# A gated linear recurrence with a feed-forward layer on one core: weights loaded in six pieces, the quarter turn by a 128-row matmul, and another order table

## The chip, the core and the metric

The kernel runs on one core of one Trainium2 chip. The core has five engines that each work through a queue of their own in order: TensorE (PE, with its weight loads shown apart as PEld), VectorE (DVE), ScalarE (ACT), GpSimd (POOL) and SyncE (SP). SP issues most transfers; sixteen DMA engines carry them out. The metric is the device time of one execution in microseconds (us); a lower number is better. The median of three runs of the kernel before is 193.87 us (193.51 to 193.95). One further execution was recorded by the hardware profiler, and all durations below are from it.

## The reference

For each of 4 batches and 8 heads a state of 48 x 48 is carried over 768 steps, with a complex decay per step and row, and a layer norm with a feed-forward layer follows on the 384 channels of each token:

```
mag = sqrt(a_re^2 + a_im^2);  scale = min(mag, 0.999) / (mag + 1e-6)
for t in range(768):
    S_re, S_im = ar*S_re - ai*S_im + k[t] v[t]^T,  ar*S_im + ai*S_re
    y[t] = q[t] @ S_re                      # x: 8 heads side by side, 384 channels
xn = (x - mean(x)) / sqrt(var(x) + 1e-6) * g_ln
out = x + max(xn @ w_ch1, 0) @ w_ch2        # w_ch1 384 x 1536, w_ch2 1536 x 384
```

Inputs and output are float32.

## The kernel before, in words

**Tiling.** The 768 steps of a batch are cut into chunks of 128 steps. Two chunks make a pair, so there are 12 pairs P (three to a batch) and 24 chunks n. Step names carry these numbers: `ln.3.0` belongs to pair 3, `y.5` to chunk 5. Pair 0 is worked in two halves of four heads (`ln.0.0`, `ln.0.1`).

**The decay of a pair.** ACT takes the logarithm of a_re (`ln`, L448) and its inverse (`iv`, L450); `r` is a_im over a_re, `r2` its square, `u` a logarithm on ACT (L462), `l` and `lc` (DVE, L466 and L469) the capped logarithm of the magnitude. PE sums it over the steps with a triangle of ones (`dec`, L477), and ACT forms `e` and `en`, its exponentials (L481). The angle goes the same way: arctan on ACT (`th`, L485), summed on PE (`ph`, L492 and L496), then `sin` (L514). For pairs 0 to 3 the cosine is a sine after a quarter turn: `qt` (L521) adds 0.25 to the sum on PE with a one-row matmul. Later pairs use `abs` and a bias. `car` hands the last angle on to the next pair.

**The attention of a pair.** `qe`, `ke`, `qs`, `ks` scale q and k by these tables (DVE or POOL, L294). `qT` and `kT` transpose on PE (L593) and `qsT`, `ksT` copy the result out (L291 on DVE, L289 on ACT), or SP does both with a transposing DMA (L598). Then `am` (L616), the mask `atm` (DVE), the state `gm` and `G`, the output `y` (L666, L669) and its copy `x`, its statistics `bn`, and its transpose `xtr` and copy `xT`.

**The feed-forward of a pair.** `mm1` (L720, 6 calls of 6 matmuls), `relu` (L731 ACT, L733 DVE), `mm2` (L741, 6 calls of 4 matmuls), the scaling and sum `oa` and `ot`, and the store `st`. The norm's gain and mean are folded into the first weight matrix once at the start: `wgc` makes a matrix of the gain, `wp` (PE, L384) the column means of a third of w1b, and nine `wc` (DVE, L388) correct w1b in place. `mm1` of a third waits for its three `wc`.

**Weights.** `wl.0` (L364) and `wl.1` (L366) load the two matrices whole. POOL issues them, because the transfer casts float32 to bfloat16. They go to a DMA queue of their own, q0 in the profile; all of SP's transfers go to q1.

**Order.** Every step and its engine stand in the table `PLAN`, written out ahead of time by a planner: `name:engine`, with the PSUM bank behind the letter and, after `@`, a step of another engine that must have ended first. The kernel issues the steps in that order, so each engine's queue is the table filtered by that engine, and a step that waits holds up everything behind it on its engine. `tab.log` and `tab.trig` (L775) load the ACT tables for logarithms and exponentials, or for sine and arctan. `warm` steps (L770) are matmuls whose results nobody reads.

Of the kernel before, what the change touches and what calls it, by code (L numbers as in the profile page):

```python
# [51 lines left out]
tab.trig.1:A sin.0.0:A3 qe.0.1.0:V qe.0.0.0:V q.1.1:S mask:G ke.0.0.0:G@qe.0.0.0 ke.0.1.0:V r2.2.0:V
qs.0.0.1:V qs.0.1.1:V th.1.0:A qt.0.1:P0 warm.52:P4 warm.53:P4 warm.54:P4 warm.55:P4 warm.56:P4 warm.57:P4
warm.58:P4 warm.59:P4 warm.60:P4 warm.61:P4 warm.62:P4 warm.63:P4 warm.64:P4 warm.65:P4 warm.66:P4
warm.67:P4 warm.68:P4 warm.69:P4 qt.0.0:P3 dps.0:P2 cos.0.0:A3 cos.0.1:A0 ks.0.0.1:V ks.0.0.0:V ks.0.1.0:V
qs.0.1.0:V ph.1.0:P4 dec.1.0:P6 qs.0.0.0:V warm.70:P1 warm.71:P1 qT.1:P3 tab.log.2:A en.1.0:A6 u.2.0:A
ln.3.0:A iv.3.0:A e.1.0:A6 v.0:G@qs.0.0.0 decc.0:V2 ks.0.1.1:V vf.1.1:S vf.1.0:S q.2.0:S car.1.0:V4
warm.72:P1 warm.73:P1 kT.0:P2 qT.0:P1 kT.1:P0 qsT.1:V3 tab.trig.2:A sin.1.0:A4 ksT.0:V2 wl.0:G ksT.1:V0
am.1:P2 gm.0:P0 ke.1.0.1:G@ks.0.1.1 ke.1.0.0:G th.2.0:A qsT.0:V1 am.0:P6 dps.1:P1 decc.1:A1 qt.1.0:P4
l.2.0:V r.3.0:V lc.2.0:V G.0:V0 gm.1:P0 cos.1.0:A4 dec.2.0:P4 k.2.1:S tab.log.3:A e.2.0:A4 en.2.0:A4  # L60
atm.0:V6 atm.1:V2 G.1:V0 r2.3.0:V k.2.0:S are.4.0:S ph.2.0:P6 y.1:P1 aim.4.0:S ks.1.0.1:G@lc.2.0 x.1:V1
are.5.0:S ks.1.0.0:G y.0:P2 kT.3:P3 x.0:V2 ksT.3:V3 u.3.0:A tab.trig.3:A sin.2.0:A6 wp.2:P0 wc.2.1:V0
wc.2.0:V0 xtr.0:P1 wl.1:G xtr.1:P4 wp.0:P5 wp.1:P2 wc.2.2:V0 xT.1:V4 qt.2.0:P6 xT.0:A1 kT.2:P3 th.3.0:A
# [12 lines left out]
ph.4.0:P0 atm.4:V2 k.4.0:S y.4:P5 mm2.2.1:P4 ks.3.0.0:G ks.3.0.1:V l.4.0:V lc.4.0:V mm2.3.0:P6 mm2.3.1:P6
gm.4:P7 mm2.3.2:P6 abs.4.0:A0 sin.4.0:A0 qe.3.0.0:V qs.3.0.0:V qs.3.0.1:V dec.4.0:P2 vf.3.1:S st.0:S G.4:V7
# [138 lines left out]
def kernel(  # L216
# [590 lines left out]
```

## Time and profile before

| what | value |
|---|---|
| median of three runs | 193.87 us |
| span of the profiled execution, first to last instruction | 191.7 us |
| PE, DVE, ACT, POOL busy in it | 175.3, 154.8, 165.2, 109.2 us |
| ACT table loads | 23, 29.5 us |
| warm matmuls | 74, 10.5 us |
| start of the first `mm1` (L720) | 37.45 us |
| w1b: issue by POOL, time to landing | 22.69 us, 9.9 us |
| w2b: issue by POOL, time to landing | 31.43 us, 11.9 us |

The profiled execution gives its span and no time of its own that includes what lies around the span; the span is 2.2 us under the median of the runs. A matmul's duration in the profile includes its way through the array, so neighbours overlap; what one costs in a dense stretch is the length of the stretch over the count.

### The profile page before, as it was taken

Reading aid. Unit: us, or ns where it says so; the run is one execution under the profiler, and the core shown is the slowest. Engines: PE = TensorE matmul, PEld = TensorE weight load, DVE = VectorE, ACT = ScalarE, POOL = GpSimd, SP = SyncE. Lnnn points to the kernel's source line nnn. Section 1 sums busy time; section 2 is a strip of 40 time slices with the busy share of each in tenths; the row PEclk is TensorE's granted clock in tenths of the full one; section 3 lists DMA queues with packets and bytes.
Section 4 is the critical chain, followed back from the end, with each engine's and each line's share of the span. In section 5 each row is a group of like instructions: output and inputs, shape, how many; then the busy total and the mean of one; then the engine's idle time right before and its main releaser. Section 6 shows DMA issues by size and latency. Waiting matters only on the chain.

```text
span 191.7 us, 5125 instructions
## 1 busy us (share of the span) xinstructions
PE 175.3 (91%) x2039; PEld 132.7 (69%) x2039; DVE 154.8 (81%) x267; ACT 165.2 (86%) x234; POOL 109.2 (57%) x124
## 2 busy tenths in 40 slices
PE   5567958999999989999999999999999999999991
PEld 3355644577786777787686877868777678787760
DVE  2369996999999998799999989997987484868612
ACT  3999999989999999999799988999999989427540
POOL 8601449927695599652496764585495857600500
PEclk9999996999999999999999999999999999999997
DMA  6999999999899979999899996999998979996033
GB/s 151 291 244 219 236 190 203 168 218 298 184 212 237 166 163 255 192 258 211 161 169 265 167 255 152 184 288 253 204 228 153 208 145 144 248 103 165 3 129 118
DMA packets 132104, 37.56 MB, mean 196 GB/s; under 512 B 127088, under 2 KB 131696, under 8 KB 132080
## 3 DMA queue, kind: packets, MB, share of 16 engines
q1 hardware_dynamic: 130128, 34.88, 87.7%
q0 software_dynamic: 1952, 2.36, 7.3%
q8 instruction: 16, 0.26, 0.5%
q14 instruction: 8, 0.07, 0.1%
HBM read 28.31 MB, written 4.72 MB: 172 GB/s over the span
## 4 chain that ended last, share of the span: by engine, by line
PE 38%; ACT 27%; DVE 16%; issue 8%; DMA 4%; POOL 3%; SPq 1%; DVEq 0%; POOLq 0%; ACTq 0%
PE banks L741 14%; PE banks L720 9%; ACT h L731 5%; ACT L775 4%; DVE w1b L388 3%; DMA qsT<-qs 3%; PE banks L477 2%; PE banks L616 2%; DVE l L466 2%; ACT r L462 2%; ACT en L481 2%; PE banks L496 2%; PE banks L593 2%; ACT r L458 2%; DMA are<-in_a_re_dram 2%
## 5 line engine op out<-in xcount | busy, mean ns | idle before, releaser
L741 PE MATMUL banks<-w2b,h 128*128 128x384 bf16 x288 | 54.9, 326 | 0.3 <-ACT h L731 0.2
L720 PE MATMUL banks<-xT,w1b 128*128 128x256 bf16 x432 | 51.9, 272 | 0.8 <-ACT trig L514 0.5
L720 PEld LDWEIGHTS <-w1b 128*128 128x128 bf16 x432 | 41.2, 98 | 7.7 <-DVE xT L291 1.3
L741 PEld LDWEIGHTS <-h 128*128 128x128 bf16 x288 | 26.0, 97 | 14.3 <-ACT h L731 0.8
L294 DVE TENSOR_TENSOR atm<-banks,mask 128x1024 bf16<-128x1024 f32 x24 | 28.7, 1217 | 5.2 <-PE banks L616 2.8
L731 ACT ACTIVATE h<-banks 128x1024 bf16<-128x1024 f32 x24 | 24.1, 1023 | 8.7 <-PE banks L720 8.5
L775 ACT ACT_TABLE_LOAD x23 | 29.5, 1283 | 1.2 <-PEq L791 0.8
L294 POOL TENSOR_TENSOR ks<-ke,trig 128x768 bf16<-128x768 bf16 x14 | 22.8, 1640 | 8.8 <-DVE ke L294 2.8
L294 POOL TENSOR_TENSOR qs<-qe,trig 128x768 bf16<-128x768 bf16 x11 | 18.0, 1641 | 12.3 <-DVE ot L755 5.0
L294 POOL TENSOR_TENSOR ke<-k,en 128x384 bf16<-128x384 f32 x18 | 16.5, 930 | 11.8 <-DMA vf<-in_v_dram 10.3
L294 POOL TENSOR_TENSOR qe<-q,e 128x384 bf16<-128x384 f32 x16 | 14.6, 921 | 12.2 <-ACT e L481 5.9
L733 DVE TENSOR_SCALAR h<-banks 128x1024 bf16<-128x1024 f32 x12 | 14.5, 1215 | 4.9 <-PE banks L720 4.9
L753 POOL TENSOR_TENSOR ot<-ot,x 128x384 f32<-128x384 f32 x8 | 7.3, 916 | 14.6 <-ACT ot L746 13.6
L616 PE MATMUL banks<-qsT,ksT 128*128 128x128 bf16 x192 | 14.3, 219 | 1.4 <-DVE ksT L291 1.2
L616 PEld LDWEIGHTS <-ksT 128*128 128x128 bf16 x192 | 12.1, 98 | 3.4 <-DVE ksT L291 1.4
L496 PE MATMUL banks<-th,u_th 128*128 128x384 f16 (+1 forms) x52 | 12.4, 325 | 2.2 <-ACT th L485 2.2
L679 DVE BATCH_NORM_STATS2 stats<-x 128x6 f32<-128x384 bf16 x24 | 13.1, 547 | 0.0
L755 DVE SCALAR_TENSOR_TENSOR ot<-banks,rstd,x 128x384 f32<-128x384 f32 x16 | 9.6, 609 | 4.1 <-DMA out_dram<-ot 2.9
L466 DVE SCALAR_TENSOR_TENSOR l<-r,w 128x768 f16<-128x768 f16 (+1 forms) x13 | 11.5, 892 | 1.6 <-ACT r L462 1.6
L770 PE MATMUL banks<-u_e 128*128 128x256 f16 x74 | 10.5, 302 | 2.2 <-POOL u_e L328 2.2
L477 PE MATMUL banks<-l,u_e 128*128 128x384 f16 (+1 forms) x52 | 10.4, 327 | 2.2 <-DVE l L469 1.3
L448 ACT ACTIVATE w<-are 128x768 f32<-128x768 f32 (+1 forms) x13 | 10.3, 796 | 2.2 <-DMA are<-in_a_re_dram 2.2
(96 smaller groups left out, 372.1 us busy)
## 6 DMA issues: line engine op xcount, KB each, us to landing
q<-in_q_dram SPq DMA_DIRECT2D x24, 192.0 KB, 4.0
k<-in_k_dram SPq DMA_DIRECT2D x24, 192.0 KB, 4.1
vf<-in_v_dram SPq DMA_DIRECT2D x24, 192.0 KB, 4.2
out_dram<-ot SPq DMA_DIRECT2D x24, 192.0 KB, 2.9
are<-in_a_re_dram SPq DMA_DIRECT2D x11, 384.0 KB, 4.4
aim<-in_a_im_dram SPq DMA_DIRECT2D x11, 384.0 KB, 4.5
w1b<-in_moe_w_ch_dram POOLq DMA_DIRECT2D x1, 1152.0 KB, 9.9
w2b<-in_moe_w_ch_dram POOLq DMA_DIRECT2D x1, 1152.0 KB, 11.9
```

Source lines behind the costliest of these rows:

```text
L294: {"DVE": nc.vector, "POOL": nc.gpsimd}[eng(name)].tensor_tensor(**kw)
L466: nc.vector.scalar_tensor_tensor(out=S_("l"), in0=S_("r2"), scalar=0.5, in1=S_("w"), op0=ALU.mult, op1=ALU.add)
L477: nc.tensor.matmul(heads(ps[:, c]), lhsT=u_e[:, c, j], rhs=step(T("l", P), j), start=(j == 0), stop=(j == R - 1))
L496: nc.tensor.matmul(heads(ps[:, c]), lhsT=u_th[:, c, j], rhs=step(T("th", P), j), start=False, stop=(j == R - 1), skip_group_check=True)
L616: nc.tensor.matmul(ps[:, h], lhsT=T("ksT", n)[:, h], rhs=T("qsT", n)[:, h], start=True, stop=True)
L679: nc.vector.bn_stats(out=T("stats", n), in_=T("x", n))
L720: nc.tensor.matmul(ps[:, jj], lhsT=w1b[:, dc, ts(gi * JG + jj, C)], rhs=T("xT", P)[:, dc].rearrange("p c t -> p (c t)"), start=(dc == 0), ...
L731: act(out=dst, in_=src, func=AF.Relu)
L733: nc.vector.tensor_scalar(out=dst, in0=src, scalar1=0.0, scalar2=None, op0=ALU.max)
L741: nc.tensor.matmul(bank(f"o.{n}")[:, 0:DM], lhsT=T("h", P)[:, j, ts(c, C)], rhs=w2b[:, j], start=(j == 0), stop=(j == NJ - 1))
L770: g.add(f"warm.{i}", lambda i=i: nc.tensor.matmul(bank(f"warm.{i}")[:, 0:256], lhsT=u_e[:, 0, 0], rhs=u_e[:, 1].rearrange("p j t -> p (j t ...
L775: g.add(f"tab.{nm}.{i}", lambda tab=tab: nc.scalar.preload_act_table_set(tab))
```

## The change

There are three edits in the code and a new table. The two weight loads become six: `wl.0` to `wl.2` load thirds of w1b (512 columns each), `wl.3` to `wl.5` thirds of w2b. `wp.i` now waits for its own third, and `mm2.n.i` for its own. The quarter turn uses all 128 rows of `pick` and `qrow`, and `qrow` is zero but for its row HALF, which takes one more memset. The table has 137 `warm` steps for 74, 15 table loads for 23, and the other steps in another order, some on other engines: among others 31 `relu` on ACT (24 before), 19 `ks` on DVE (12), 7 `r2` on DVE (4), 27 transposing DMAs (25), and 21 `qT` and `kT` on PE (23).

```
-    g.add("qrow", lambda: nc.gpsimd.memset(qrow[ds(HALF, 1)], 0.25), needs=["ue"])
+    g.add("qrow", lambda: [nc.gpsimd.memset(qrow, 0.0), nc.gpsimd.memset(qrow[ds(HALF, 1)], 0.25)],
+          needs=["ue"])
-    g.add("wl.0", lambda: nc.gpsimd.dma_start(
-        out=w1b, in_=moe_w_ch1.rearrange("(dc p) j -> p dc j", p=C)))
-    g.add("wl.1", lambda: nc.gpsimd.dma_start(
-        out=w2b, in_=moe_w_ch2.rearrange("(jc p) e -> p jc e", p=C)))
+    for i in range(NG):
+        g.add(f"wl.{i}", lambda i=i: nc.gpsimd.dma_start(
+            out=w1b[:, :, ts(i, 512)], in_=moe_w_ch1.rearrange("(dc p) j -> p dc j", p=C)[:, :, ts(i, 512)]))
+        g.add(f"wl.{NG + i}", lambda i=i: nc.gpsimd.dma_start(
+            out=w2b[:, ts(i, JG)], in_=moe_w_ch2.rearrange("(jc p) e -> p jc e", p=C)[:, ts(i, JG)]))
-        g.add(o, wp, needs=["wgc", "wl.0"], ps=(o, 1))
+        g.add(o, wp, needs=["wgc", f"wl.{jb}"], ps=(o, 1))
-                        nc.tensor.matmul(ps[:, c], lhsT=pick[ds(HALF, 1)], rhs=qrow[ds(HALF, 1), 0:W],
+                        nc.tensor.matmul(ps[:, c], lhsT=pick, rhs=qrow[:, 0:W],
-                    needs=[f"relu.{P}.{part}", "wl.1"] + ([f"mm2.{n}.{part - 1}"] if part else []),
+                    needs=[f"relu.{P}.{part}", f"wl.{NG + part}"] + ([f"mm2.{n}.{part - 1}"] if part else []),
-    for i in range(240):
+    for i in range(137):
```

The table itself is replaced as a whole. This is what each queue does up to about the first `mm1`, taken from the old and the new table by filtering them by engine (bank numbers left out):

```
ACT before: tab.log.0 ln.1.0 iv.1.0 ln.0.0 iv.0.0 ln.0.1 iv.0.1 tab.trig.0 th.0.1 r2.0.0 th.0.0 sin.0.1
  tab.log.1 u.0.0 u.0.1 u.1.0 ln.2.0 iv.2.0 en.0.0 en.0.1 e.0.1 e.0.0 tab.trig.1 sin.0.0 th.1.0 cos.0.0 cos.0.1
  tab.log.2 en.1.0 u.2.0 ln.3.0 iv.3.0 e.1.0 tab.trig.2 sin.1.0 th.2.0 decc.1 cos.1.0 tab.log.3 e.2.0 en.2.0 u.3.0
  tab.trig.3 sin.2.0 xT.0 th.3.0 cos.2.0
ACT after:  tab.log.0 ln.0.1 iv.0.1 ln.0.0 iv.0.0 u.0.1 u.0.0 ln.1.0 e.0.1 iv.1.0 ln.2.0 en.0.1 iv.2.0 e.0.0
  u.1.0 en.0.0 tab.trig.1 th.0.0 th.0.1 th.1.0 sin.0.0 sin.0.1 th.2.0 cos.0.0 cos.0.1 tab.log.2 u.2.0 ln.3.0 e.1.0
  iv.3.0 en.1.0 tab.trig.3 sin.1.0 th.3.0 cos.1.0 tab.log.4 e.2.0 u.3.0 ln.4.0 en.2.0 iv.4.0 tab.trig.5 sin.2.0
  x.1 xT.0 sin.3.0 cos.2.0
DVE after:  uth r.0.1 r2.0.1 r.0.0 r2.0.0 l.0.1 lc.0.1 l.0.0 lc.0.0 r.1.0 r2.1.0 r.2.0 wgc l.1.0 r2.2.0 lc.1.0
  qe.0.1.0 qe.0.0.0 ke.0.1.0 ke.0.0.0 car.0.0 car.0.1 ks.0.0.1 ks.0.1.1 qs.0.1.1 wc.0.0 wc.0.2 wc.1.0 wc.1.1 wc.0.1
  l.2.0 qs.0.0.1 car.1.0 lc.2.0 qsT.0 decc.0 ksT.0 decc.1 ksT.1 wc.2.1 wc.1.2 wc.2.0 atm.0 qsT.1 wc.2.2 G.0 x.0
  atm.1 G.1 qs.1.0.1 ks.1.0.1 ks.1.0.0 qsT.3 ksT.2 xT.1
POOL after: ue mask ident car0.1 cmean pad.qs.1 one pad.qs.2 car0.0 zdec wl.0 pick qrow pad.ks.0 wl.1@lc.0.0
  pad.qs.0 wl.2 pad.ks.1 ks.0.0.0@qs.0.1.1 qs.0.0.0 ks.0.1.0 qs.0.1.0 r.3.0@lc.2.0 r2.3.0 qe.1.0.1 qe.1.0.0 v.0
  qs.1.0.0 ke.1.0.0 ke.1.0.1 wl.3 wl.4 pad.ks.2 wl.5
SP before:  are.1.0 are.0.0 gln are.0.1 aim.0.1 aim.0.0 aim.1.0 are.2.0 q.0.0 aim.2.0 k.0.0 q.2.1 q.0.1 k.0.1
SP after:   are.0.1 are.0.0 aim.0.1 aim.0.0 are.1.0 are.2.0 aim.1.0 aim.2.0 q.0.1 gln q.0.0 k.0.1 k.0.0
PE after:   warm x46 dec.0.1 warm dec.0.0 warm x53 ph.0.0 ph.0.1 dps.0 wp.0 qt.0.0 qt.0.1 ph.1.0 wp.1 dec.1.0
  warm x23 qT.0 kT.0 kT.1 dps.1 wp.2 dec.2.0 qt.1.0 am.0 qT.1 warm x12 gm.0 y.0 am.1 ph.3.0 gm.1 ph.2.0 xtr.0 y.1
  qT.3 warm x2 kT.2 qt.2.0 xtr.1 qT.2 kT.3 mm1.0.2.0 mm1.0.2.1
```

In the old table PE does `ph.3.0`, `qT.2` and `qT.3` after the first two calls of `mm1`, not ahead of them; `wl.0` stands behind `v.0` on POOL, and `wl.1` behind `ks.1.0.0`.

## Prediction

> **What bounds the kernel now.** I read the summary of busy time first, then the busy time by stretches, then the chain of work that ended last, and last the DMA queues and the timelines around the weight loads. The page gives shares of the span and, in tenths, how busy 40 slices were:
>
> ```profile
> PE 175.3 (91%) x2039; PEld 132.7 (69%) x2039; DVE 154.8 (81%) x267; ACT 165.2 (86%) x234; POOL 109.2 (57%) x124
> PE   5567958999999989999999999999999999999991
> PEclk9999996999999999999999999999999999999997
> ```
>
> PE is loose only in the first seven or eight slices. Two stretches, split at the first `mm1`, say it sharper (PE, PEld, DVE, ACT, POOL busy, then clock, DMA share, GB/s):
>
> ```profile
> 0.00:37.45 37.45, 26.84 (x274) 18.74 (x274) 27.16 (x53) 33.87 (x48) 20.86 (x42) 0.95 1.03 213
> 37.45:187.50 150.05, 148.23 (x1766) 113.99 (x1766) 126.76 (x214) 131.32 (x187) 88.38 (x83) 1.00 0.96 194
> ```
>
> Busy is not yet full speed, so I priced the matmuls by dense stretches of the chain (start, length, what, count):
>
> ```profile
> 99.31 0.65 PE banks L477 x4
> 163.37 0.45 PE banks L616 x8
> 179.86 3.93 PE banks L720 x36
> 183.79 3.92 PE banks L741 x24
> 187.73 0.62 DVE ot L755
> ```
>
> That is 109 ns for a matmul of `mm1`, 163 ns for `mm2`, `dec` and `ph`, 56 ns for a transpose or `am`. With the y and gm blocks at 25 ns (16 in about 0.41 us), the whole list of non-warm matmuls comes to about 163 us, of which some 14 lie before 37.45. The remaining 149 fill the 150 us up to 187.5. So from the first `mm1` on, PE runs without a hole, and the span is *start of mm1 + what PE still has to do + 4.2 us* (187.5 to the span's end of 191.7: last `ot`, last store). ACT and DVE keep some 20 us of slack in that stretch.
>
> What the weight loads do to the others is seen in the queues (packets, MB, share of 16 engines' time). Without a weight load, 10 to 18 us:
>
> ```profile
> q1 hardware_dynamic: 9017, 1.87, 112.0%
> ```
>
> In 25 to 32 us, while w1b is loaded, and then the issues that were under way just before it (22.7 to 24.9 us; last column us from issue to landing):
>
> ```profile
> q0 software_dynamic: 397, 1.18, 89.4%
> q1 hardware_dynamic: 1126, 0.21, 18.3%
> ...
> vf<-in_v_dram SPq DMA_DIRECT2D x1, 192.0 KB, 10.7
> q<-in_q_dram SPq DMA_DIRECT2D x1, 192.0 KB, 10.0
> k<-in_k_dram SPq DMA_DIRECT2D x1, 192.0 KB, 11.2
> ```
>
> The page's medians for the same loads are 4.0 to 4.2 us. While the weights move, SP's queue gets 0.03 MB/us instead of 0.23, and everything in it lands 6 to 7 us late. In the kernel before nothing needed soon was in that queue.
>
> ```profile
> 22.69 1.00 POOL L364 DMA_DIRECT2D w1b<-in_moe_w_ch_dram  x1
> 24.05 8.44 SPq L404 DMA_DIRECT2D k<-in_k_dram  x2
> ```
>
> **Part 1, w1b moved to the start.** On POOL `wl.0` now follows `ue` and nine short steps. By POOL's rows (`ue` ends at 2.1; mask 0.57, ident 0.52, two car0 0.36 each, two pads 0.47 each, cmean, `one` and zdec 0.37) it is issued at 5.2. In the rows above the issue at 22.69 has moved no byte of q0 by 24.9 and is at full rate from 25, so the pieces move from about 7.5. `wl.1` waits for `lc.0.0` (8.4), `wl.2` follows 1.5 us later; both are queued before the piece ahead is through. How long the three hold the engines no row shows. In one piece w1b took 9.9 us from issue, 7.6 of them moving (384 packets); w2b 11.9, 9.9 of them moving (1536 packets). Three pieces are 1152 packets; bounds 7.5 and 10 us, and I take 8.8, between the two. So until 16.3 SP's queue is starved. It moves 0.03 to 0.05 MB/us then (in 34 to 42 us, during w2b, q0 moved 1416 packets and q1 1481, 0.42 MB: packet for packet).
>
> What stands in it: all of pair 0's, 1's and 2's a_re and a_im, 2.36 MB up to `aim.2`. By 7.5 us 1.50 MB have moved (the window up to 7.5), so 0.86 are left; 0.44 go during the weights, 0.42 after them at 0.25 to 0.28 MB/us. `aim.2` has landed at about 18.6, against 11.3 without weights. `aim.1` lands at about 16.5, against 9.5.
>
> Who waits: on ACT `u.1.0` (behind `r.1.0`, `r2.1.0`) until 18, and with it `en.0.0`, `tab.trig.1` and every `th`; on DVE `r.1.0`, `r.2.0`, and behind those `wgc`, `l.1.0`, all of pair 0's `qe`, `ke`, `car`. DVE then has a closed list from `r.2.0` to `xT.1`, at the pitch of its rows: r.2.0 0.95, wgc 0.6, l.1.0 0.9, r2 and lc 0.9, four qe/ke 2.0, two car 0.7, three halves of ks/qs 0.9, five wc 3.4, l.2.0 to lc.2.0 2.1, qsT.0, ksT.0, ksT.1 and two decc 2.45, three wc 2.0, atm.0, qsT.1 and wc.2.2 2.5, G.0, x.0, atm.1, G.1 2.7, three qs/ks 1.7, qsT.3, ksT.2, xT.1 1.6. The sum is 25.4 us, without holes, so `xT.1` ends and `mm1.0.2.0` starts at 18.6 + 25.4 = 44.0 us. ACT's list reaches `xT.0` at about 43 by the same adding, POOL's r.3.0 to ke.1.0.1 ends near 40.5: DVE's is the last. Without starvation l.1.0 could start when u.1.0 ends, at 13.9, and `mm1` at 13.9 + 23.9 = 37.8. With the bounds 7.5 and 10 us, and 0 to 1 us of holes in DVE's list, `mm1` starts at 42.5 to 46.
>
> **Part 2, what PE has left.** Ahead of `mm1` the new order has also `ph.3.0` (6 x 163 ns) and `qT.2`, `qT.3` (16 x 56 ns): 1.9 us less afterwards. Two `qT` fewer in all: 0.9 us less. Left 150.05 - 2.8 = 147.3 us.
>
> **Part 3, warm matmuls.** 63 more at 107 ns (2.67 us for 23), all ahead of `mm1` where PE waits: nothing. Should they stand in front of late work, 12 x 0.107 = 1.3 us at most. The 53 before `ph.0.0` end near 15.4, and `th.0.0` comes at about 21. In the trace gaps near 28 to 29 us were followed by a granted clock of 0.86 in the stage 30 to 40. The Trainium skill (TensorE: Matmul & The Clock Gate, "Part 1: The HAM clock gate") says the clock halves after an idle window of about 3.4 us; the trace agrees in kind, and by that rule some 2 us of PE work doubles here, which DVE's list covers.
>
> **Part 4, eight table loads fewer.** 8 x 1.283 = 10.3 us off ACT; seven more `relu` (7 x 1.02) and other exchanges (r2, ksT, rstd, decc off it, qsT, oa on it) leave ACT 10 to 11 us lighter, at about 155, DVE at about 156 (8.5 us of relu off it, ks, qs, r2, decc, ksT on it), POOL at about 101. After `mm1` starts, none of the three reaches PE's 147 us. So the gain I count is 0; its cover is PE, and if PE were not full it would be up to 2.8 us (8/23 of the 8.1 us that L775 has in the chain).
>
> **Part 5, small things.** The 128-row quarter turn: 323 ns (1 row) against 351 ns (L492, 128 rows), ten matmuls, 0 to 0.3 us, in gaps; I take 0. The extra qrow memset, 0.42 us on POOL between `wl.0` and `wl.1`: 0. Four more DMA issues at 1.0 to 1.08 us: `wl.3` to `wl.5` stand together (3.2 us) before qe.2, ke.2; the last third of w2b lands near 54, when `mm2.1.2` (44.0 + about 9.8) wants it: 0 to 1 us, I take 0. Two more DMA transposes (1.3 us of issue each), 0 to 2.6, hidden in SP's slack: 0.
>
> **Sum.** 44.0 + 147.3 + 4.2 = 195.5 us of span against 191.7: +3.8. On the median that is 193.87 + 3.8 = 197.7 us. The likeliest case's own range is 196.0 to 200.0 (`mm1` at 42.5 to 46, and up to 0.3 of the rest).
>
> **Rivals.**
> *No starvation that matters (faster).* Thin pieces leave SP's queue its rate. If it keeps more than 0.13 MB/us from 7.5 us on, `aim.2` lands before 14.8 and `mm1` starts before 40.2, which is where loss and gain cancel (40.2 + 147.3 + 4.2 = 191.7). With `mm1` at 37.8 the span is 189.3 and the time 191.5. For: the pieces are smaller. Against: 0.21 MB in 7 us. Chance 0.11.
> *The pieces pass quickly (faster).* If the three hold the engines 2.7 us and not 8.8, SP's queue is back at 10.2 with 0.72 MB left, `aim.2` lands near 13.6, `mm1` starts at 39.0, and the time is 192.7. Against: w1b's 7.6 us moving, 89.4% of the engines' time for 7 us. Chance 0.05. Such a price follows from the Trainium skill (DMA: Bandwidth & Descriptors, "Anatomy of one DMA"), which fits a transfer from POOL as 2.0 us and bytes over 436 GB/s; w1b would land after 4.7 us by it, and the trace has 9.9, so the measurement decides here.
> *Table loads were on the path (faster).* The chain before gives L775 4.2% of the span. Then PE holes shrink, and with an unharmed start 191.5 - 2.8 = 188.7. Against: PE's 149 us in 150. Chance 0.05. The rule for it is in the Trainium skill (ScalarE: Activation LUTs, "Table sets: the hidden batching unit"): do all of one set before switching. Its 2.7 us a load would make 21 us; the rows have 1.283 us.
> *PE is not kept full afterwards (slower).* The new order on DVE or the exchanges of buffers leave PE 2.5% of holes after 44 us: +3.7 more, 201.4. For: 31 `relu` on one engine, 27 transposes in a DMA queue whose share is already 0.96. Against: lighter ACT. Chance 0.17.
> *Between*, `mm1` at 39.8 to 40.6: no change. Chance 0.06.
>
> **How the numbers follow.** My forecast has 0.56. A measurement of this kernel tells about 0.2% (0.4 us). Slower: 0.56 + 0.17 = 0.73; faster 0.11 + 0.05 + 0.05 = 0.21; same 0.06. The range leaves out the outer part of both sides, a tenth each: 191.3 to 201.5.
>
> **What would show it.** In the trace after: q1 near 0.05 MB/us in 8 to 16 us; DVE idle before `r` (L294) for a DMA of aim, ACT idle before L462; PE idle from about 15 to 21 us with a lower clock in 20 to 30; first L720 near 44, and then PE dense to the end, 147 us later. The prediction is wrong if the first L720 starts before 40, or if PE after it takes over 150 us.

## The result, and the profile after

The changed kernel takes 204.27 us (median; 203.94 to 206.31) against 193.91 (193.51 to 194.5): a ratio of 1.0553, 95% interval 1.0503 to 1.0602. It was forecast slower, at 197.7 us and at most 201.5, so the direction was right and the size too small by 6.6 us. Medians and ratios below leave out executions that took over 1.5% more than the fastest of their kernel. The profiled execution took 204.28 us with a span of 202.6. Line numbers are five higher than before: `mm1` is L725, `mm2` L746, the table loads L780.

The chain that ended last by engine, of the kernel before, and then from the page of the changed kernel: busy time, busy tenths of the span in 40 slices, the same chain, and the group of table loads.

```profile
PE 38%; ACT 27%; DVE 16%; issue 8%; DMA 4%; POOL 3%; SPq 1%; DVEq 0%; POOLq 0%; ACTq 0%
```

```profile
PE 181.3 (90%) x2086; PEld 138.7 (68%) x2086; DVE 159.5 (79%) x280; ACT 156.5 (77%) x215; POOL 105.0 (52%) x127
...
PE   5895299889999979999998987999999999899992
...
PEclk9999669999999999999999999999999999999999
...
PE 28%; DVE 23%; SPq 15%; DMA 14%; ACT 8%; issue 5%; POOL 5%; DVEq 0%; POOLq 0%; ACTq 0%
...
L780 ACT ACT_TABLE_LOAD x15 | 19.2, 1283 | 1.0 <-PEq L796 0.8
```

PE's first nines come later, and single 8s and 7s stand between those that follow. The chain, 38% PE and 27% ACT before, is now 28% PE, 23% DVE, and 29% SP's queue and DMA. Two stretches of the changed kernel, split at the first `mm1` (columns as before: PE, PEld, DVE, ACT, POOL busy, clock, DMA share, GB/s):

```profile
0.00:46.67 46.67, 35.65 (x358) 27.02 (x359) 30.61 (x60) 33.66 (x47) 27.32 (x52) 0.93 1.01 211
46.67:198.95 152.28, 145.65 (x1731) 111.63 (x1728) 128.31 (x220) 122.88 (x168) 77.69 (x76) 1.00 0.91 183
```

The first `mm1` starts at 46.67 us, 9.2 later than before (37.45); the forecast had 44.0. From there to the start of the last matmul PE takes 152.0 us (before 149.9), where the forecast had 147.3 to the end of its work. Priced matmul by matmul at the dense pitches of the prediction, the work left at the first `mm1` is 145.6 us before and 142.8 after. These are estimates: by the median distance from one start to the next, the work left before is 144.1 us, so the level of the gaps is uncertain by some 1.5 us, and the difference between two kernels by less. The rest of each stretch is gaps: 4.3 us before, 9.2 after. So 9.2 later, 2.8 us less work, 4.9 us more gaps and 0.5 less at the end make the 10.8 us of span.

**Where the start went.** The chain of the changed kernel (start, length, what), and DVE's timeline (start, length, instruction, in brackets the idle time before it and who ended it):

```profile
8.03 3.19 SPq L409
11.26 8.79 DMA gln<-in_moe_g_ln_dram
```

```profile
12.70 0.96 DVE L297 TENSOR_TENSOR r<-aim,are 128x768 f16<-128x768 f32 x1 [2.87 <-DMA aim<-in_a_im_dram]
...
14.17 0.95 DVE L297 TENSOR_TENSOR r<-aim,are 128x768 f16<-128x768 f32 x1
20.14 0.68 DVE L380 TENSOR_SCALAR gc<-cmean,gln 128x128 bf16<-128x128 f32 x3 [5.02 <-DMA gln<-in_moe_g_ln_dram]
```

`r.2.0` starts at 14.17 and not at 18.6, for `aim.2` landed at 13.8. Then `wgc` (the last row) waits 5.0 us for `gln`, 1.5 KB, which lands 8.8 us after its issue. In the old order `gln` stands third in SP's queue, in the new one tenth. The queues between 8 and 16 us (packets, MB, share of 16 engines' time):

```profile
q0 software_dynamic: 907, 0.90, 68.4%
q1 hardware_dynamic: 3304, 1.06, 52.7%
```

SP's queue moved 0.13 MB/us, not 0.05, and the weight pieces were through at 19.4 us, not 16.3. The 0.13 is no even rate. The pieces moved in bursts: `wl.1` was issued at 10.14 us, when the first piece was nearly through, and its bytes came from 12.4 on. From 8.2 to 10.2 us, and then in the pause from 10.4 to 12.4:

```profile
q0 software_dynamic: 342, 0.34, 104.0%
q1 hardware_dynamic: 242, 0.09, 17.7%
...
q1 hardware_dynamic: 1592, 0.60, 109.6%
q0 software_dynamic: 29, 0.02, 8.3%
```

Beside a moving piece SP's queue got 0.045 MB/us, as forecast, and in the pause 0.30.

**Where the gaps come from.** The two longest gaps of PE after the first `mm1`, 1.14 and 1.84 us, on the timelines of PE, DVE and POOL of the changed kernel:

```profile
71.11 1.95 DVE L297 TENSOR_TENSOR ks<-ke,trig 128x768 bf16<-128x768 bf16 x1
...
70.84 1.81 POOL L297 TENSOR_TENSOR r<-aim,are 128x768 f16<-128x768 f32 x1 [2.38 <-ACT are L455]
...
75.25 0.61 PE L598 MATMUL banks<-ident,ks 128*128 128x128 bf16 x8 [1.14 <-DVE qsT L294]
...
117.92 2.18 DVE L471 SCALAR_TENSOR_TENSOR l<-r,w 128x768 f16<-128x768 f16 x1
120.25 1.45 DVE L297 TENSOR_TENSOR r<-aim,are 128x768 f16<-128x768 f32 x1
121.62 1.06 DVE L474 TENSOR_SCALAR l<-l 128x768 f16<-128x768 f16 x1
...
117.65 1.64 POOL L297 TENSOR_TENSOR qs<-qe,trig 128x768 bf16<-128x768 bf16 x1
119.25 3.21 POOL L297 TENSOR_TENSOR ke<-k,en 128x384 bf16<-128x384 f32 x2
...
122.74 0.81 PE L482 MATMUL banks<-l,u_e 128*128 128x384 f16 x4 [1.84 <-DVE l L474]
```

Elsewhere in this trace the same `ks` takes 0.54 us, `l` 0.95, `r` 0.95, `lc` (L474) 0.35. Each long one lies beside an instruction of POOL: the `ks` ends at 73.06, 0.4 us after POOL's `r` does (72.65).

### The profile page after: what moved, and what is told of

Same layout as the page of the kernel before. It is cut to its first block, busy times and chain, and to the rows that moved or that the text cites. A ratio compares the mean times of both kernels' runs of the same rounds, so it can differ in the third digit from the quotient of the medians.

```text
span 202.6 us, 5230 instructions
## 1 busy us (share of the span) xinstructions
PE 181.3 (90%) x2086; PEld 138.7 (68%) x2086; DVE 159.5 (79%) x280; ACT 156.5 (77%) x215; POOL 105.0 (52%) x127
## 4 chain that ended last, share of the span: by engine, by line
PE 28%; DVE 23%; SPq 15%; DMA 14%; ACT 8%; issue 5%; POOL 5%; DVEq 0%; POOLq 0%; ACTq 0%
PE banks L746 9%; PE banks L725 9%; SPq L409 6%; SPq L450 5%; DVE atm L297 5%; DMA gln<-in_moe_g_ln_dram 4%; DMA q<-in_q_dram 4%; DVE ks L297 3%; DMA vf<-in_v_dram 2%; SPq L603 2%; DMA k<-in_k_dram 2%; DVE w1b L393 2%; DMA aim<-in_a_im_dram 2%; ACT h L736 2%; PE banks L621 2%
## 5 line engine op out<-in xcount | busy, mean ns | idle before, releaser
L746 PE MATMUL banks<-w2b,h 128*128 128x384 bf16 x288 | 55.8, 326 | 0.0
L725 PE MATMUL banks<-xT,w1b 128*128 128x256 bf16 x432 | 51.6, 273 | 0.5 <-ACT ot L751 0.4
L725 PEld LDWEIGHTS <-w1b 128*128 128x128 bf16 x432 | 41.3, 98 | 6.5 <-issue 0.8
L736 ACT ACTIVATE h<-banks 128x1024 bf16<-128x1024 f32 x31 | 31.4, 1026 | 4.9 <-PE banks L725 4.6
L746 PEld LDWEIGHTS <-h 128*128 128x128 bf16 x288 | 25.4, 97 | 12.7 <-ACT h L736 0.3
L297 POOL TENSOR_TENSOR qe<-q,e 128x384 bf16<-128x384 f32 x18 | 16.9, 948 | 12.0 <-DVE l L471 8.2
L297 POOL TENSOR_TENSOR ks<-ke,trig 128x768 bf16<-128x768 bf16 (+1 forms) x7 | 10.9, 1552 | 18.4 <-DVE qs L297 15.3
L780 ACT ACT_TABLE_LOAD x15 | 19.2, 1283 | 1.0 <-PEq L796 0.8
L775 PE MATMUL banks<-u_e 128*128 128x256 f16 x137 | 17.4, 286 | 2.3 <-POOL u_e L331 2.2
L775 PEld LDWEIGHTS <-u_e 128*128 128x128 f16 x137 | 13.9, 103 | 4.5 <-POOL u_e L331 1.9
L758 POOL TENSOR_TENSOR ot<-ot,x 128x384 f32<-128x384 f32 x10 | 9.4, 941 | 14.3 <-ACT ot L751 12.1
L297 DVE TENSOR_TENSOR r<-aim,are 128x768 f16<-128x768 f32 (+1 forms) x9 | 8.4, 928 | 6.9 <-DMA aim<-in_a_im_dram 6.8
L297 DVE TENSOR_TENSOR ks<-ke,trig 128x768 bf16<-128x768 bf16 (+1 forms) x19 | 12.9, 697 | 1.0 <-POOL ke L297 0.9
L467 ACT ACTIVATE r<-r,one_b 128x768 f16<-128x768 f16 (+1 forms) x13 | 11.5, 888 | 2.6 <-DVE r L297 2.5
L297 POOL TENSOR_TENSOR qs<-qe,trig 128x768 bf16<-128x768 bf16 (+1 forms) x8 | 11.8, 1479 | 1.9 <-DVE qs L297 1.7
```

The lines of the kernel that those rows point to most:

```text
L297: {"DVE": nc.vector, "POOL": nc.gpsimd}[eng(name)].tensor_tensor(**kw)
L467: add(f"u.{X}", lambda S_=S_: act(out=S_("r2"), in_=S_("r2"), func=AF.Ln, bias=one_b), needs=[f"r2.{X}", "one"], uses=[("r2", P)])
L725: nc.tensor.matmul(ps[:, jj], lhsT=w1b[:, dc, ts(gi * JG + jj, C)], rhs=T("xT", P)[:, dc].rearrange("p c t -> p (c t)"), start=(dc == 0), ...
L736: act(out=dst, in_=src, func=AF.Relu)
L746: nc.tensor.matmul(bank(f"o.{n}")[:, 0:DM], lhsT=T("h", P)[:, j, ts(c, C)], rhs=w2b[:, j], start=(j == 0), stop=(j == NJ - 1))
L775: g.add(f"warm.{i}", lambda i=i: nc.tensor.matmul(bank(f"warm.{i}")[:, 0:256], lhsT=u_e[:, 0, 0], rhs=u_e[:, 1].rearrange("p j t -> p (j t ...
```

## The experiments

All kernels that gave a time, "PE" being the time from the first `mm1` to the start of the last matmul in the profiled execution, and "gaps" that time less the priced work left (145.6 us in the old order, 142.8 in the new, 144.6 in the two with a shorter DVE list). Gaps hold what a lower granted clock costs, too: in this stretch it was 0.50 for 3.4 us in "four waits on POOL" and twice for 3.4 us in "before, eight loads more", and 1.00 in the others. A profiled execution can lie up to 1.4 us from the median of its kernel.

| run | us | ratio to before (95%) | first mm1 | PE | gaps |
|---|---|---|---|---|---|
| before | 193.91 | 1 | 37.45 | 149.9 | 4.3 |
| changed | 204.27 | 1.0553 (1.0503-1.0602) | 46.67 | 152.0 | 9.2 |
| before, code edits alone | 193.95 | 0.9984 (0.9968-1.0000) | 37.98 | 150.1 | 4.5 |
| before, w1b early | 198.41 | 1.0218 (1.0166-1.0271) | 40.91 | 150.0 | 4.4 |
| before, no waits between engines | 196.79 | 1.0150 (1.0104-1.0195) | 37.74 | 151.9 | 6.3 |
| before, loads repeated | 193.91 | 1.0005 (0.9987-1.0022) | 38.47 | 149.8 | 4.2 |
| before, eight loads more | 203.20 | 1.0472 (1.0437-1.0507) | 39.14 | 158.5 | 12.9 |
| changed, w1b later | 201.37 | 1.0377 (1.0342-1.0412) | 44.23 | 151.8 | 9.0 |
| changed, gln first | 202.68 | 1.0439 (1.0406-1.0473) | 45.04 | 153.0 | 10.2 |
| changed, w1b, wp and wc later | 202.40 | 1.0465 (1.0430-1.0500) | 44.22 | 151.2 | 8.4 |
| the same, two loads moved | 202.13 | 1.0462 (1.0377-1.0547) | 44.66 | 150.7 | 7.9 |
| changed, two waits on POOL | 202.10 | 1.0418 (1.0357-1.0479) | 47.91 | 150.0 | 7.2 |
| shorter DVE list | 200.31 (one) | none | 38.40 | 156.3 | 11.7 |
| shorter DVE list, all cures | 200.73 | 1.0305 (1.0283-1.0327) | 40.82 | 154.8 | 10.2 |
| four waits on POOL | 202.65 | 1.0394 (1.0315-1.0474) | 43.68 | 153.4 | 10.6 |
| changed, eight loads more | 209.95 | 1.0850 (1.0804-1.0896) | 47.95 | 156.4 | 13.6 |

Not in the table is the changed kernel with the two loads moved alone; its times stand in its own section. The shorter DVE list has one time and no ratio: its four executions took 200.31, 204.12, 204.21 and 205.12 us. No row shows why.

### The code edits alone

The old table with the six weight loads at the places of the two, and the 128-row quarter turn.

```
-wl.0:G
+wl.0:G wl.1:G wl.2:G
...
-wl.1:G
+wl.3:G wl.4:G wl.5:G
```

> The old order table with the two code edits alone: six weight pieces, issued where the two loads stood, and the 128-row quarter turn. If the order of the table is what costs, this stays within 0.3% of 193.9 us and the first mm1 starts at 37 to 38.5 us. If smaller pieces or the 128-row quarter turn cost by themselves, it loses 1% or more.

0.9984 with a first `mm1` at 37.98 us. In the old order the code costs nothing that can be told; the change's price comes with the table.

### The early weight load alone, in the old order

```
 pad.qs.0:G
+wl.0:G
...
-wl.0:G
```

> The old kernel with one step moved: w1b's load (still whole) is issued by POOL at about 5 us instead of 22.7. If a weight load in the first 20 us starves SP's queue and SP's data set the start, the loads of q, k and the third pair land 5 to 8 us late, the first mm1 starts at 41 to 45 us, and the time is 197.5 to 201 us. If the start is set by the length of the engines' lists and not by transfers, the first mm1 stays at 37 to 38.5 us and the time at 193.9.

198.41 us, 4.2 more than the 194.22 beside it, first `mm1` at 40.91. DVE's timeline and the DMA issues of this kernel in 7 to 17 us:

```profile
18.09 0.96 DVE L287 TENSOR_TENSOR r<-aim,are 128x768 f16<-128x768 f32 x1 [2.20 <-DMA aim<-in_a_im_dram]
```

```profile
aim<-in_a_im_dram SPq DMA_DIRECT2D x1, 384.0 KB, 11.0
```

Here the mechanism of the prediction is seen in its plain form: `aim.2` takes 11.0 us and lands at 18.0, where it landed at 11.8 before. From 8 to 14.8 us, with w1b moving in one piece, SP's queue gets 0.38 MB, 0.056 MB/us: close to the rate that the prediction took. The first `mm1` moves by 3.5 us, and the 150.0 us after it do not change. The start also holds more time at a granted clock of 0.50 (20.7 to 27.5 and 34.3 to 37.8 us; before, 29.3 to 32.7 alone), and no run separates the two.

### The weight load later, in the new order

```
-wl.0:G ... wl.1:G@lc.0.0 ... wl.2:G
 r.2.0:V
+wl.0:G@r.2.0 wl.1:G wl.2:G
```

> The changed kernel with one thing altered: the three pieces of w1b wait on POOL for r.2.0, so that they start at about 12 us, behind the loads of pairs 0 to 2. Starvation theory: gln lands at about 12.5 us in place of 20, the first mm1 starts at 38 to 41 us in place of 46.7, what follows still takes 152 us, and the time is 195.5 to 198.5 us. Rival, that the new lists of DVE and ACT are too long by themselves: first mm1 at 45 us or later, 202.5 to 204.5 us.

201.37 us: 2.9 less than the changed kernel, not the 6 to 9 expected. The first `mm1` comes at 44.23, 2.4 us earlier. SP's loads are on time now, but a new wait takes their place. PE's and DVE's timelines:

```profile
21.06 0.59 PE L384 MATMUL banks<-w1b,gc 128*128 128x512 bf16 x1 [3.53 <-DMA w1b<-in_moe_w_ch_dram]
...
22.54 1.41 DVE L388 SCALAR_TENSOR_TENSOR w1b<-w1b,gln,banks 128x512 bf16<-128x512 bf16 x2 [2.99 <-PE banks L384]
26.43 2.06 DVE L388 SCALAR_TENSOR_TENSOR w1b<-w1b,gln,banks 128x512 bf16<-128x512 bf16 x3 [2.49 <-PE banks L384]
```

`wp.0` stands ahead of `qt.0.0` in PE's list, so the late w1b holds up the angles, and the `wc` on DVE wait with it.

### gln earlier in SP's queue

```
-gln:S
 aim.0.0:S
+gln:S
```

> The changed kernel with the small load of g_ln moved from the tenth to the fifth place in SP's queue. If that load alone holds up DVE (5.0 us of waiting), the first mm1 comes 4 to 5 us earlier and the time is 199 to 200.5 us. If all of SP's queue is late, DVE waits for q and k of pair 0 instead, which landed at 20.7 and 22.4 us: the first mm1 comes 0.5 to 1.5 us earlier and the time is 202.5 to 204 us.

202.68 us, 1.6 less. `gln` was the load that DVE's wait names, but the q and k behind it are late as well: `qe` now waits 0.9 us for q until 20.64 and `ke` 0.6 us for k. What is late is the queue.

### Weight load, wp and wc later

```
+wl.0:G@r.2.0 wl.1:G wl.2:G         (behind r.2.0)
-dps.0 wp.0 qt.0.0 qt.0.1 ph.1.0 wp.1 dec.1.0 ... dps.1 wp.2 dec.2.0 qt.1.0 am.0 qT.1
+dps.0 qt.0.0 qt.0.1 ph.1.0 dec.1.0 wp.0 ... dps.1 wp.1 dec.2.0 qt.1.0 am.0 qT.1 wp.2
-qs.0.1.1 wc x5 l.2.0 qs.0.0.1 car.1.0 lc.2.0 ... ksT.1 wc x3 atm.0 qsT.1 wc G.0
+qs.0.1.1 l.2.0 qs.0.0.1 car.1.0 wc x3 lc.2.0 ... ksT.1 wc x3 atm.0 qsT.1 wc x3 G.0
```

> The changed kernel with w1b's three pieces issued behind r.2.0 (as in the run with that edit alone) and, besides, the three products wp and the nine w1 corrections wc that use them put later in PE's and DVE's lists: wp.0 behind dec.1.0, wp.1 behind dps.1, wp.2 behind am.0. Theory (the start loses 9.2 us to the weight load alone: SP's loads late when it comes early, qt and dec late behind wp.0 when it comes late): with both cured DVE's list of 25.4 us runs nearly without a hole from 13.3, first mm1 at 38.5 to 41.5, PE after it as before this edit (151.8 to 152.3), time 195.5 to 199. Rival (the new order of the start is itself slower, by the holes at cos and wgc that have other causes): first mm1 at 43 to 45, time 200.5 to 202.5.

First `mm1` at 44.22, as in the run before last, and 202.40 us, no better than its 201.37: the theory that the weight load was the whole of the start falls. The wait on w1b is gone and another shows, on DVE for ACT behind a table load:

```profile
19.70 1.28 ACT L775 ACT_TABLE_LOAD   x1
21.00 0.94 ACT L462 ACTIVATE r<-r,one_b 128x768 f16<-128x768 f16 x1
...
21.96 1.25 DVE L466 SCALAR_TENSOR_TENSOR l<-r,w 128x768 f16<-128x768 f16 x1 [2.38 <-ACT r L462]
```

From 21.96 DVE is busy almost without a break up to `xT.1` at 43.1. With SP's loads on time the new order still starts its first `mm1` 6.8 us later than the old one, of which 2.8 are work that PE has then behind it.

### Loads earlier in SP's queue

```
-vf.4.1:S are.7.0:S vf.3.0:S st.0:S q.4.1:S ksT.6:S k.5.0:S k.4.0:S st.2:S vf.4.0:S
+are.7.0:S vf.3.0:S st.0:S q.4.1:S ksT.6:S k.5.0:S k.4.0:S st.2:S vf.4.1:S vf.4.0:S
...
-ksT.13:S ksT.12:S aim.9.0:S
+aim.9.0:S ksT.13:S ksT.12:S
```

> The changed kernel with two loads moved in SP's list: vf.4.1, which waits there 5.9 us for v.2, goes behind k.4.0, and aim.9.0 goes ahead of the two transposes ksT.13 and ksT.12. Theory (after first mm1 PE takes 152.0 us where 147.1 us of work were left, since loads queued on SP behind waiting DMAs come late): q.4.1 lands by 67 instead of 72.6, aim.9.0 by 117 instead of 120.1, the holes of 1.3 us at 73.8 and of 2.0 us at 120.7 close, PE from the first mm1 to the last matmul 149.5 to 151, time 202 to 203.3; first mm1 unchanged at 46.7. Rival (the lists of DVE and ACT set the holes, the loads are only late in step with them): 203.7 to 204.7, the holes open again elsewhere, PE 151.7 to 152.5.

Its executions took 202.65 to 207.57 us (ratio 1.0532, 1.0434 to 1.0630): no gain that can be told. The edit did less than it should, for the next in the queue waits in the same place, the store `st.0` for its `ot`. SP's timeline, in the execution of 207.57 us:

```profile
59.07 2.27 SPq L404 DMA_DIRECT2D vf<-in_v_dram  x1
69.48 0.36 SPq L761 DMA_DIRECT2D out_dram<-ot  x1
69.89 0.43 SPq L404 DMA_DIRECT2D q<-in_q_dram  x1
```

> Both edits above together in the changed kernel: w1b's pieces later with wp and wc later, and the two loads moved in SP's list. If both theories hold the gains add: first mm1 at 38.5 to 41.5 and PE 149.5 to 151 after it, time 193 to 198. If only the start is right: 195.5 to 199. If neither: 200 to 204.

With both edits: 202.13 us, PE 150.7 against 151.2 without the two loads moved. `q.4.1` lands 1.3 us earlier and `aim.9.0` 2.1 us earlier, and the two long gaps stand where they were, at 1.13 and 2.26 us. Late loads on SP are not what makes these two gaps.

### Two waits on POOL

```
-r.6.0:G
+r.6.0:G@ks.3.0.1
...
-qs.7.0.1:G
+qs.7.0.1:G@lc.8.0
```

> The changed kernel with two waits added on POOL alone: r.6.0 behind DVE's ks.3.0.1, and qs.7.0.1 behind DVE's lc.8.0. Ahead of the two longest holes of PE after the first mm1 (1.3 us at 73.8, 2.0 us at 120.7) DVE's instructions are stretched while POOL works beside them: ks 1.95 us instead of 0.54, l 2.18 instead of 0.95, r 1.45 instead of 0.95, lc 1.06 instead of 0.35. Theory (the new order lays POOL's work beside DVE's at these places and so holds up PE): the stretched ones take their short times, both holes shrink by 1 us or more each, PE from first mm1 to last matmul 149 to 150.3 instead of 152.0, time 201.5 to 203. Rival (the holes come from late loads or from the order of DVE's list, or POOL's own later work takes up the gain): 203.7 to 205, PE 151.5 to 152.5.

202.10 us and PE 150.0, both as the theory had it. DVE, POOL and PE at the two places:

```profile
72.36 0.55 DVE L292 TENSOR_TENSOR ks<-ke,trig 128x768 bf16<-128x768 bf16 x1
...
73.04 1.81 POOL L292 TENSOR_TENSOR r<-aim,are 128x768 f16<-128x768 f32 x1 [3.33 <-DVE ks L292]
...
118.29 0.95 DVE L466 SCALAR_TENSOR_TENSOR l<-r,w 128x768 f16<-128x768 f16 x1
...
121.26 0.35 DVE L469 TENSOR_SCALAR l<-l 128x768 f16<-128x768 f16 x1
...
121.67 0.81 PE L477 MATMUL banks<-l,u_e 128*128 128x384 f16 x4 [0.50 <-DVE l L469]
```

With POOL held back, DVE's instructions have their short times, the first gap is gone and the second is 0.50 us instead of 1.84. These two waits alone take 2.2 us off the time, and the intervals of the two ratios do not overlap, though the profiled execution started its `mm1` 1.2 us later. Of the gaps 2.0 us go; another one, before L616, has grown from 0.50 to 1.14 us (at 174.0).

### A shorter DVE list before the first mm1

On top of "weight load, wp and wc later":

```
-wl.0:G@r.2.0 wl.1:G wl.2:G
+wl.2:G@r.2.0 wl.0:G wl.1:G
-l.2.0 qs.0.0.1 car.1.0 wc.0 x3 lc.2.0 ... ksT.1 wc.1 x3 atm.0 qsT.1 wc.2 x3 G.0 x.0 atm.1 G.1 qs.1.0.1 ks.1.0.1 ks.1.0.0 qsT.3 ksT.2 xT.1
+qs.0.0.1 car.1.0 wc.2 x3 l.2.0 lc.2.0 ... ksT.1 atm.0 qsT.1 G.0 x.0 atm.1 G.1 qs.1.0.1 wc.0.0 xT.1 wc x5 ks.1.0.1 ks.1.0.0 qsT.3 ksT.2
-tab.trig.5 sin.2.0 x.1 xT.0        (ACT)
+x.1 xT.0 tab.trig.5 sin.2.0
-warm.123 ... warm.136
```

`wp` on PE follows the same order, and the first two calls of `mm1` go ahead of `qT.3`, `kT.2`, `qT.2` and `kT.3`.

> On top of the run with w1b's pieces later and wp and wc moved: what DVE does ahead of the first mm1 is cut back to what the kernel before did there. Piece 2 of w1b is loaded, multiplied and corrected first (the first two mm1 read that piece alone), the six corrections wc.0 and wc.1, ks.1.0.0, ks.1.0.1, qsT.3 and ksT.2 go behind xT.1, l.2.0 goes behind wc.2, x.1 and xT.0 go ahead of the table load on ACT, and the 12 warming matmuls ahead of gm.0 are left out. Theory (the new order of the start is slower by itself, because DVE has 30.6 us from r.2.0 to xT.1, of them six corrections 4.1, two ks 2.5, two evictions 1.4, a wait of 2.4 for ACT): first mm1 at 36.5 to 40 instead of 44.2, PE after it 150 to 153, time 192.5 to 198. Rival (DVE's list is only beside another limit of the start, ACT's list with its table loads or POOL's r.3.0; or the deferred work holds up PE by as much afterwards): first mm1 at 41 to 44, or PE after it 155 to 159; 199 to 203 either way.

First `mm1` at 38.40, within a microsecond of the kernel before; yet the time is 200.3 us and the span only 0.7 us shorter than without the edit. PE's timeline, and the stretch after the first `mm1`:

```profile
38.40 1.47 PE L718 MATMUL banks<-xT,w1b 128*128 128x256 bf16 x12
...
41.23 0.62 PE L591 MATMUL banks<-ident,ks 128*128 128x128 bf16 x8 [0.91 <-DVE ks L290]
```

```profile
38.40:194.73 156.33, 147.99 (x1761) 113.58 (x1759) 133.14 (x227) 124.01 (x170) 77.01 (x76) 1.00 0.96 190
```

What was taken out of the start comes back right after it: PE 156.3, gaps 11.7. The second pair's `mm1` starts at 55.0 us here, at 56.2 without the edit and at 53.1 before. From the first `mm1` to there are 16.6 us, without the edit 12.0; of the 4.6 us more, 1.8 are the four transposes (32 x 56 ns) that now come later, and the rest are waits. The expectation's rival named this; the place of the first `mm1` is no measure of the start.

> The run before this one with POOL's two waits and the two loads moved in SP's list besides. If all theories hold: first mm1 at 36.5 to 40, PE after it 148.5 to 151, time 190.5 to 196: level with the kernel before or below it. If only the start is right: 192.5 to 198; if neither: 199 to 203.

With POOL's two waits and the two loads moved besides: 1.0305. This is the lowest ratio in the new order, still 5.9 us above the kernel before by the ratio and 6.6 by the medians (200.73 against 194.15). Its executions spread from 199.87 to 203.75 us.

### More waits on POOL

On top of "the same, two loads moved": POOL's two waits, and two more.

```
-r.6.0:G ... qs.7.0.1:G ... qe.4.0.0:G ... r.11.0:G
+r.6.0:G@ks.3.0.1 ... qs.7.0.1:G@lc.8.0 ... qe.4.0.0:G@lc.5.0 ... r.11.0:G@ks.9.0.0
```

> The run with w1b's pieces later and wp and wc moved (202.4 us, PE 151.2 from first mm1 to last matmul), with both loads moved in SP's list and four waits on POOL: the two of the run with waits alone, qe.4.0.0 behind DVE's lc.5.0, and r.11.0 behind ks.9.0.0. Theory (most of the idle PE time that the new order adds after the first mm1 comes from DVE instructions stretched beside POOL, and with these four places and the late aim.9.0 cured PE is kept as full as in the kernel before): PE from first mm1 to last matmul 147.8 to 149.3, time 198.5 to 200.5. Rival (the rest is many short waits from the order of the lists themselves, which move when one is closed): PE 149.4 to 151, time 200.5 to 202.5.

The ratio, 1.0394, cannot be told from the 1.0462 without the waits, for their intervals overlap. In the profiled execution PE takes 153.4, 2.7 us more than the 150.7 without them, and outside what either theory expected. At one place POOL's step is itself wanted early. POOL, ACT and PE where `r.11.0` was held back:

```profile
151.20 1.81 POOL L292 TENSOR_TENSOR r<-aim,are 128x768 f16<-128x768 f32 x1 [2.52 <-DVE ks L292]
...
153.04 0.84 ACT L485 ACTIVATE th<-r 128x768 f16<-128x768 f16 x1 [2.53 <-POOL r L292]
...
153.93 0.49 PE L496 MATMUL banks<-th,u_th 128*128 128x384 f16 x2 [1.84 <-ACT th L485]
```

Behind this gap, from 154.9 to 158.3 us, the granted clock is 0.50, and 31 matmuls of `mm1` take 5.09 us, 164 ns each instead of 109: some 1.7 of the 2.7 us are the clock. A wait cures a collision where POOL has slack, and opens a gap where it has none. No run found one cause for the rest of the gaps.

### The kernel before without its waits between engines

```
-ke.4.0.0:G@lc.5.0 ... qe.6.0.1:G@ke.6.0.0 ... v.6:G@ks.6.0.0
+ke.4.0.0:G ... qe.6.0.1:G ... v.6:G
...                                  (all 23 alike)
```

> The kernel before with all its 23 waits of one engine's work behind the other's left out of the table (the @ parts; what the data need stays). Theory (where POOL works beside DVE, DVE's 16-bit instructions are stretched, and these waits keep that off the path): DVE's time over its short durations rises from 6.8 us to 12 or more, PE gets holes of a microsecond, time 195.5 to 201. Rival (the stretch costs nothing in this order because PE has other work beside it, or what POOL gains by starting earlier makes up for it): 193 to 195.2.

196.79 us, 1.0150. DVE's time over its short durations (each instruction against the shortest of its form) is 10.4 us instead of 6.7; 12 was expected. The changed kernel has 11.2; the code edits alone have 8.4 at an unchanged time, so a stretch costs only where something waits for it. The longest gap, with DVE's timeline, POOL's and PE's:

```profile
91.50 2.45 DVE L284 TENSOR_TENSOR qs<-qe,trig 128x768 bf16<-128x768 bf16 x2
...
94.25 1.61 DVE L284 TENSOR_TENSOR ke<-k,en 128x384 bf16<-128x384 f32 x1
...
91.31 2.23 POOL L284 TENSOR_TENSOR qe<-q,e 128x384 bf16<-128x384 f32 x2 [3.58 <-DMA q<-in_q_dram]
93.61 1.83 POOL L284 TENSOR_TENSOR qs<-qe,trig 128x768 bf16<-128x768 bf16 x1
...
96.51 0.32 PE L482 MATMUL banks<-car,pick 128*128 128x384 f16 x1 [1.23 <-DVE car L499]
```

In the kernel before the same two `qs` take 1.02 us together and `ke` 0.55. So the cause that cost the changed kernel 2 us is at work in the old order too, held down there by the waits.

### What table loads are worth

A first run named each extra load's table right behind the load of that same table.

```
 tab.log.2:A
+tab.log.20:A
...                                  (eight such)
```

> The kernel before with eight of its 23 table loads done twice in a row (31 loads, 10.3 us more on ACT, spread over pairs 1 to 9). Theory (table loads lie beside PE's work, as the prediction costed their saving at nothing): 193.6 to 195.2. Rival (they are on the path, since ACT is busy 131 of the 150 us after the first mm1): 1.28 us each, 198 to 204; and then the change's eight fewer loads should have been worth some us.

Its trace has 23 loads, as before: the loads that name the table in place are not in it. The run is a repetition of the kernel before, at 1.0005. The second changes the table and back:

```
 tab.log.3:A
+tab.trig.20:A tab.log.20:A
...                                  (behind tab.log.5, 7 and 9 too)
```

> The kernel before with eight more table loads: behind the loads tab.log.3, 5, 7 and 9 ACT loads the table for sine and then the one for logarithms once more (31 loads, 10.3 us more on ACT, in four lumps of 2.6 us). In the earlier run each extra load named the table that was in place already, and none was carried out. Theory (table loads lie beside PE's work, as the prediction costed their saving at nothing): 193.6 to 196, the lumps costing 0 to 2 us in all. Rival (ACT's loads are on the path of the dense part): 10.3 us more or a good part of it, 198 to 204; then eight loads fewer should have been worth some us in the changed kernel.

203.20 us, 1.0472: 10.3 us of loads make the time 9.2 us longer, and the rival is right. PE's gaps go from 4.3 to 12.9 us. The granted clock in tenths and the chain by engine, with ACT at 31% where it was 27%:

```profile
PEclk9999985999999979999999699999999999999999
...
PE 39%; ACT 31%; DVE 14%; issue 6%; DMA 5%; POOL 3%; SPq 1%; POOLq 0%; DVEq 0%; ACTq 0%
```

Not all of the 9.2 us is waiting for ACT. Behind two of PE's gaps the granted clock is 0.50 for 3.4 us (from 70.1 and from 111.0 us), which makes up to 3.4 of the 8.6 us more of gaps. It is the smaller part: the execution with the highest mean clock, 0.991, still took 202.47 us, the profiled one with 0.966 took 203.83.

The mirror of it in the changed kernel:

```
 tab.log.4:A
+tab.trig.20:A tab.log.20:A
...                                  (behind tab.log.6, 8 and 10 too)
```

> The changed kernel with eight more table loads in four lumps of 2.6 us, behind tab.log.4, 6, 8 and 10 (23 loads, as many as the kernel before). Theory A (the new order has moved the path off ACT: 8% of the chain that ended last against 27% before, and ACT idles for PE and DVE): most of the 10.3 us lie beside other work, 204.5 to 208, and the saving of eight loads was never going to be worth much in this order. Theory B (ACT is on the path as in the kernel before, where the same lumps cost 9.2 us): 211 to 215, and then the change gains some 9 us by its fewer loads and its other parts lose close to 20.

209.95 us, 5.7 more than the changed kernel, between the two theories. The gaps grow by 4.4 us, all of it in the first five pairs; the last extra load ends at 120.6, and from the sixth pair on (first `mm1` at 121.0) the time left is as without the loads, 83.3 us. Here the granted clock stays at 1.00 after the first `mm1`. So ACT is on the path of the new order in its first half; behind that nothing was added. Eight loads are worth up to 5.7 us to it in these places. If the eight that the change leaves out are worth as much, which no run shows, its other parts lose 16 us, nearly three times the gain.

## Why the prediction was right or wrong

**Part 1, the weights at the start: the mechanism is there, its size and its load are wrong.** The starvation costs 4.2 us in the old order and 2.9 in the new. The step that failed is "`aim.2` has landed at about 18.6". SP's queue kept 0.13 MB/us instead of 0.05, so `aim.2` landed at 13.8. But the pieces were under way until 19.4 us instead of 16.3, and the next in the queue, `gln` and the first q, landed at 20. The forecast gave neither of them a landing time. Behind the 18.6 stands "both are queued before the piece ahead is through": POOL issued `wl.1` at 10.14, behind a wait for `lc.0.0`, so the pieces left a pause of 2 us in which SP's queue moved 0.60 MB. The rate beside a moving piece was about right: 0.045 and 0.06 MB/us in 8.2 to 10.2 and 12.4 to 14.4 us. The Trainium skill (DMA: Bandwidth & Descriptors, "Queues, rings and completion order") states that a DMA engine takes turns between the queues it has work for, packet by packet. The trace of the early load in the old order agrees: 182 packets of weights to 186 of SP's in 10 to 13 us. In the changed kernel's bursts the counts differ more, 342 to 242 and 319 to 345.

DVE's "closed list" of 25.4 us gives 20.1 + 24.4 = 44.6 from `wgc` on; 46.67 is 2.1 more, by waits, 1.5 us of them for ACT, and stretched instructions. That 44.0 was only 2.7 us off is luck: the forecast was 6.2 us of starvation on a start of 37.8, and the runs show 2.4 us on a start of 44.2.

**Rival "No starvation that matters": wrong by more than its condition.** Its bound of 0.13 MB/us was just about reached, as an average over bursts and a pause, and it did not help, because the load that mattered was another one. It also had the start without starvation at 37.8. The two kernels with SP's loads on time and DVE's list kept long start their `mm1` at 44.2: in one DVE waits 5.5 us for the products `wp` of the late w1b, in the other 2.4 us for ACT behind a table load, and its `l` and `ks` are stretched.

**Part 2: right.** By count and pitch, the work left at the first `mm1` fell by 2.8 us (145.6 to 142.8).

**"PE runs without a hole", the step that failed most.** The 147.3 us after the first `mm1` were 152. The prediction took 149 us of work in 150 us; recounted, it was 145.6, so the kernel before had 4.3 us of gaps already. The new order has 9.2. The rival "PE is not kept full afterwards" came true, and gave 201.4 by 3.7 us of gaps; there were 4.9 more. Some 2 us of the 9.2 are shown by the two waits on POOL: DVE's instructions stretched beside POOL's. The prediction did not look for this, though the trace of before has such rows. The Trainium skill (SBUF — State Buffer, "SBUF: two separate sides") states that DVE and GpSimd share a port pair, and that whichever starts first holds it for its whole instruction, where DVE is in a two-port mode, or has two SBUF inputs beside a GpSimd instruction that reads SBUF. The trace agrees: the `ks` and the `l` above end 0.4 and 0.8 us after the POOL instruction beside which they started, near their own 0.54 and 0.95, while `atm`, which reads PSUM, takes 1.21 to 1.23 us throughout.

**Part 4, table loads at zero: wrong.** Its cover was that "none of the three reaches PE's 147 us". Slack in a sum over 150 us was no cover: eight loads put into the kernel before cost 9.2 us, and into the new order 5.7, where the forecast had 2.8 at most. The chain had hinted at it: ACT held 27% of it. The error had the other sign, and so hid part of the loss elsewhere. The rival that had the table loads on the path was right in that, and the kernel is slower all the same.

**Parts 3 and 5: the code edits cost 0, as forecast.** The 63 warm matmuls alone were not tried. They did not keep the clock up: the slices at 20 to 30 us show 6 tenths, as the forecast had it. This is not the 10 us: the execution with the highest mean clock, 0.992, took 203.94 us.

**What stays open.** 2.9 us for the early weights and 2.2 for the two collisions are shown, each by a run of its own, and a gain of up to 5.7 from the table loads stands against them. The change costs 10.4 us, so if these add, some 11 us more lie in the new order itself; the run with all cures, 5.9 us above the kernel before by its ratio, fits that. They are spread over the start (the first `mm1` at 44.2 even with loads on time, and little gain from pulling it forward) and over gaps of 0.2 to 1.1 us, which moved when one was closed. The exchanges between engines (`relu` to ACT, `ks` and `r2` to DVE, two more transposing DMAs) were not tried alone. So the cause of the larger part stays open: the runs show that it comes with the table, but not which of its moves it is.

## What to carry to other kernels

An engine's slack over a long stretch is no cover for work on it: add the work at the place in question and see what arrives in the time; here 10.3 us of loads cost 9.2 us on an engine that was 86% busy, in part through a lower clock of another engine. When a transfer starves a queue, look past the load that you think decides to the next ones in it, and look at the rate burst by burst, for an average over a window hides the pauses. When an order is changed, look for DVE's work on SBUF beside POOL's, and do not judge a start by its first large matmul: work put behind it may be waited for just the same.

## What the runs showed of the hardware

- DVE's `ks` took 1.95 us beside POOL's `r` and 0.54 to 0.55 us without; `l` 2.18 and 0.95; `lc` 1.06 and 0.35.
- A 1.5 KB load took 8.8 us to land, behind other loads of its queue and while 1.2 MB of weights moved in another one. Beside a moving piece of weights its queue moved 0.045 to 0.06 MB/us, in the pause between two pieces 0.30.
- ACT table loads that name the table in place are not in the trace (31 written, 23 there); those that change it took 1283 ns each time.
- The granted clock fell to 0.50 for 3.4 us right behind gaps of PE of 1.83 us and of 1.32 and 0.63 us in one run (eight loads more) and of 1.84 us in another (four waits on POOL). It stayed at 1.00 behind gaps of 1.84 and 2.26 us in two others (changed; the same, two loads moved).
